# Batch 0's first feed-forward matrix in three token groups inside its own attention, with the weights loaded earlier and the scores ordered anew

## The chip, the cores and the metric

The kernel runs on one core of one Trainium2 chip. The time is that of the device, in microseconds (us), from start to end of one execution. Other numbers come from the profile of one execution of each kernel.

Names of the engines: PE is the tensor engine (matmuls), DVE the vector engine, ACT the scalar engine, POOL the GpSimd engine, SP the engine that issues most DMAs here. A **step** is one pass of the kernel's main loop and handles two score tiles. There are 180 steps, 22.5 for each of 8 batches.

## The reference, cut to what matters

```python
# q, k, v: (8, 12, 448, 64); w_pre, w_post: (12, 12)
scores = q @ k.T / 8                       # per batch and head, 448 x 448
scores = einsum('bhij,hg->bgij', scores, w_pre)     # mix the heads
attn = softmax(scores)
attn = einsum('bhij,hg->bgij', attn, w_post)        # mix the heads again
x = (attn @ v) as (3584, 768)
h = max(x @ w_in, 0)                       # w_in: 768 x 2048
out = (h * h) @ w_out                      # w_out: 2048 x 768
```

For each batch there is attention, which uses all engines, and then a feed-forward part, which is mostly PE work. Its weights are the same for all batches.

## The kernel before

The main loop software-pipelines the attention. Scores of a block of 120 queries are computed (`s_ps`), evicted to an SBUF tile `S` by ACT and DVE, gathered by DMA into tiles `G` that hold 12 heads x 10 queries, mixed (`m_ps`), exponentiated on ACT (`e_sb`), normalised on POOL (`d`), mixed back and transposed (`at_ps`), and multiplied by V (`ot_ps`). The tile `S` has two buffers, so the first evictions of block n+2 wait for the last gathers of block n. Feed-forward work is "filler": it is put between attention instructions of the *next* batch, at an even rate, because PE and POOL run in program order here.

```python
def ffn1_unit(b, ft):
    ps = bank("h_ps")
    for c2 in range(NPAIR):
        nc.tensor.matmul(ps[:, 0:S], lhsT=w1[...], rhs=xts[b][:, c2, :], ...)
    h2 = ffnp.tile([P, S], BF16, name="h2", tag="h2", bufs=FT + 1)
    hr = ffnp.tile([P, S], F32, name="hr", tag="hr", bufs=2)
    nc.scalar.activation(out=hr[:, :], in_=ps[:, 0:S], func=ACT.Relu)
    nc.gpsimd.tensor_tensor(out=h2[:, :], in0=hr[:, :], in1=hr[:, :], op=ALU.mult)
    h2ts[(b, ft)] = h2
# ... cut ...
for x in range(8):                                    # loads, by tile index
    at_load(9 + 5 * x if x else 8, load_w1, x)
    at_load(52 + 2 * x, load_w2, x)
# ... cut ...
for ds in range(nd + LAG):                            # the steps
    # ... loads due, transposes of the next batch due ...
    for s in now2:
        mix(s)
    fill(share)                                       # some filler
    # ... cut: timed units, each charged to the filler's account (owed) ...
    if old2:
        unmix(old2)
        for b1, t1 in old2:
            # ... cut: attention times V when a part of the tiles is done ...
            if t1 == NT - 1:                          # all of batch b1 done
                at_step(ds + 1, (0, lambda b1=b1: filler.extend(ffn_units(b1))))
    for i in (2 * ds + AHEAD, 2 * ds + AHEAD + 1):
        if i < len(steps):
            gather(steps[i])
    scores_up_to(2 * ds + AHEAD + 2)
    fill(share)
```

The softmax here doesn't subtract the row's maximum and nothing guards it: scores larger than these inputs give would overflow.

Of the kernel before, what the change touches and what calls it, by code (L numbers as in the profile page):

```python
# [36 lines left out]
TURN = {0: (6, 8), 1: (7, 8 + LAG), B: (2, 8 + LAG)}  # L37
# [4 lines left out]
def kernel(  # L42
# [24 lines left out]


# [155 lines left out]
    def ffn1_unit(b, ft):  # L224
        ps = bank("h_ps")
        for c2 in range(NPAIR):
            nc.tensor.matmul(ps[:, 0:S], lhsT=w1[ft // 4][:, c2, ft % 4 * 128:ft % 4 * 128 + 128], rhs=xts[b][:, c2, :],  # L227
                             start=(c2 == 0), stop=(c2 == NPAIR - 1))
        h2 = ffnp.tile([P, S], BF16, name="h2", tag="h2", bufs=FT + 1)
        hr = ffnp.tile([P, S], F32, name="hr", tag="hr", bufs=2)  # L230
        nc.scalar.activation(out=hr[:, :], in_=ps[:, 0:S], func=ACT.Relu)  # L231
        nc.gpsimd.tensor_tensor(out=h2[:, :], in0=hr[:, :], in1=hr[:, :], op=ALU.mult)  # L232
        h2ts[(b, ft)] = h2
# [38 lines left out]
    def ffn_units(b):  # L272
        u = [(1140, lambda ft=ft: ffn1_unit(b, ft)) for ft in range(FT)]
        for mt, nt in [(mt, nt) for mt in range(3) for nt in range(2)] + [(3, 0)]:
            for part in range(2):
                u.append((1310, lambda mt=mt, nt=nt, part=part: ffn2_unit(b, mt, nt, part)))
        return u
# [3 lines left out]
    def score_burst(b, blk, pairs):  # L281

        if (b, blk) not in Sb:
            Sb[(b, blk)] = work.tile([P, H, S], BF16, name="S", tag="S", bufs=2)
        sb = Sb[(b, blk)]
        got = []
        for p in pairs:
            for hh in range(2):
                rs = slice(64 * hh, 64 * hh + 64)
                ps = bank("s_ps")  # L290
                nc.tensor.matmul(ps[:, 0:S], lhsT=qTs[b][rs, p, BLK_START[blk]:BLK_START[blk] + P],  # L291
                                 rhs=kTs[b][rs, p, :], start=True, stop=True)
                got.append((2 * p + hh, ps))
        for h, ps in got:
            if h % 2 == 0 or (b == 0 and h in (3, 9)):
                nc.scalar.copy(out=sb[:, h, :], in_=ps[:, 0:S])  # L296
            else:
                nc.vector.tensor_copy(out=sb[:, h, :], in_=ps[:, 0:S])  # L298
# [14 lines left out]
    def mix(s):  # L313
        n = rows_of(s[1])
        ps = bank("m_ps")
        nc.tensor.matmul(ps[:, 0:S], lhsT=pre[0:n, :], rhs=Gs.pop(s)[0:n, :], start=True, stop=True)  # L316
        e = work.tile([P, S], F32, name="e_sb", tag="E", bufs=3)
        sm = work.tile([P, 1], F32, name="sm", tag="sm", bufs=4)
        nc.scalar.activation(out=e[:, :], in_=ps[:, 0:S], func=ACT.Exp, scale=SCALE, accum_out=sm[:, 0:1])  # L319
        rc = work.tile([P, 1], F32, name="rc", tag="rc", bufs=4)  # L320
        nc.vector.reciprocal(out=rc[:, :], in_=sm[:, :])  # L321
        d = dts[(NT * s[0] + s[1]) % ND]
        nc.gpsimd.tensor_scalar(out=d[:, 0:S], in0=e[:, :], scalar1=rc[:, 0:1], scalar2=-1.0 / S,  # L323
                                op0=ALU.mult, op1=ALU.add)
        dsb[s] = d
# [50 lines left out]
    with tc.manual_schedule(engines={PE, POOL}):  # L376
        for x in range(4):
# [3 lines left out]
            if x > 0:  # L381
                score_burst(0, 0, [2 * x - 2, 2 * x - 1])
        for x in range(2):
            score_burst(0, 1, [3 * x, 3 * x + 1, 3 * x + 2])
        for x in range(AHEAD):
            gather(steps[x])
# [5 lines left out]

        for x in range(3):
            load_v(0, x)
            at_load(48 + x, load_v, 1, x)
        for x in range(6):
            at_load(3 * x - 6 if x > 1 else -1, load_qk, 1, x)
            at_load([45, 46, 47, 53, 55, 57][x], load_qk, 2, x)
        for x in range(8):
            at_load(9 + 5 * x if x else 8, load_w1, x)  # L400
            at_load(52 + 2 * x, load_w2, x)
# [9 lines left out]
        issued = [2 * NPAIR]  # L411

        def scores_up_to(tile):
# [3 lines left out]
            size = starts[blk + 1] - starts[blk]  # L417
            want = NPAIR * (blk + 1) + -(-NPAIR * (tile - starts[blk]) // size)
            while issued[0] < want:
                score_burst(*blocks[issued[0] // NPAIR], [issued[0] % NPAIR])  # L420
                issued[0] += 1

        for f in loads.get(-1, []):
            f()
        for ds in range(nd + LAG):
# [12 lines left out]
            rest = ((NT + 1) // 2 + LAG - ds) % (NT / 2) + 1  # L438
            share = sum(w for w, _ in filler) / rest / 2 if now2 else 1e9
            now = timed.pop(ds, [])  # L440
            for s in now2:
                mix(s)
# [4 lines left out]
            if old2:  # L447
                unmix(old2)
                for b1, t1 in old2:
                    ends = PARTS[b1 % 2]  # L450
                    if t1 + 1 in ends:
                        for u in av_units(b1, ends.index(t1 + 1) - 1):
                            at_step(ds + 1, u)
                    if t1 == NT - 1:
                        at_step(ds + 1, (0, lambda b1=b1: filler.extend(ffn_units(b1))))
            for i in (2 * ds + AHEAD, 2 * ds + AHEAD + 1):
                if i < len(steps):
                    gather(steps[i])
            scores_up_to(2 * ds + AHEAD + 2)
# [36 lines left out]
```

## Time and profile before

The first three runs took 638.35, 638.35 and 638.39 us.

The first lines are from the profile page: the busy share of the span in 40 slices (tenths; 9 is 90% or more) for PE, then the granted PE clock in tenths of full speed, then the busy share of the DMA engines.

```profile
PE   4558678699999999999999999999999999999897
...
PEclk9675686799999999999999999999999999999899
DMA  9884869997655785578646885488543655432002
```

There are two regimes. In the first eight slices (to about 128 us) PE is below 90% busy and, but for the first slice, below full clock; from there almost to the end it is busy with hardly a break.

The next view is the table of stretches. Its columns are: stretch, length, busy time of PE, PEld (weight loads), DVE, ACT and POOL, each with a count of instructions, then the granted clock, the DMA share and GB/s. The stretches are cut at the starts of POOL's first `d` pass of steps 0, 12, 30, 60 and 179. POOL makes exactly two such passes in a step.

```profile
22.40:64.20 41.80, 28.44 (x373) 14.37 (x374) 23.16 (x63) 22.97 (x72) 20.32 (x32) 0.61 0.68 127
64.20:119.00 54.80, 36.91 (x505) 17.59 (x504) 35.69 (x96) 33.11 (x104) 35.53 (x54) 0.73 0.94 164
119.00:219.80 100.80, 99.61 (x1260) 53.27 (x1259) 71.86 (x176) 71.04 (x211) 75.92 (x106) 0.98 0.72 130
219.80:581.60 361.80, 355.49 (x4697) 194.43 (x4694) 265.86 (x668) 253.91 (x769) 248.09 (x355) 1.00 0.60 112
581.60:637.80 56.20, 49.23 (x387) 28.37 (x385) 9.74 (x18) 10.78 (x24) 16.15 (x18) 0.95 0.15 43
```

From step 30 on PE is busy 99 and 98% of the time. There, PE work taken away is time saved. In steps 12 to 30 it is busy 67% (36.91 of 54.80) at a clock of 0.73.

The timeline of PE shows its long stops (the first is before step 12, the others are in steps 12 to 30; columns: start, length, engine, line, operation; in brackets PE's idle time before it and what ended it):

```profile
49.40 0.96 PE L162 MATMUL tr_ps<-ident,qst 112*64 112x112 bf16 x16 [6.66 <-ACT S L296]
...
81.12 3.41 PE L181 MATMUL ot_ps<-at,v 112*64 112x160 bf16 x48 [5.89 <-ACT S L296]
...
118.25 0.58 PE L344 MATMUL at_ps<-post,d 60*128 60x60 bf16 x16 [5.22 <-ACT S L296]
...
119.28 2.42 PE L227 MATMUL h_ps<-xt,w 128*128 128x448 bf16 x6
```

PE stands still three times for 5 to 7 us until ACT evicts a score into `S` (L296). The chain of work that ended last has a gather in front of each such eviction (5.11 us before the first, 3.83 and 9.29 us before the others). The last of them (start, length, what):

```profile
108.28 9.29 DMA G<-S
...
117.66 0.54 ACT S L296
```

And the first feed-forward matmul (L227) comes only at 119.28 us: until then none is put between the attention instructions.

### The profile page before, as it was taken

The numbers are of one execution on the slowest core, as the hardware profiler recorded it, in microseconds if no ns is written. First come the engines' busy times: TensorE is split into PE (matmuls) and PEld (weight loads), VectorE is DVE, ScalarE is ACT, GpSimd is POOL, SyncE is SP. The second block draws the span as 40 slices with busy tenths as digits, with TensorE's granted clock in tenths as the row PEclk, the third lists the DMA queues.
The fourth block names the chain that finished last, engine by engine and source line by source line (L and its number), as shares of the span: only waits on it lengthen the run. The fifth ranks groups of instructions, "written<-read, shape, count | busy, mean of one in ns | idle before, by whom it ended". The sixth has DMA issues, their size and how long they took to land.

```text
span 637.8 us, 19148 instructions
## 1 busy us (share of the span) xinstructions
PE 580.7 (91%) x7338; PEld 313.8 (49%) x7338; DVE 414.9 (65%) x1050; ACT 403.5 (63%) x1196; POOL 405.7 (64%) x583
## 2 busy tenths in 40 slices
PE   4558678699999999999999999999999999999897
PEld 3125234345555456455555455545555555555454
DVE  3366666566777767777787677776787677755101
ACT  3656567477467865887578756886587757862330
POOL 6343558699448963888468943897387746873350
PEclk9675686799999999999999999999999999999899
DMA  9884869997655785578646885488543655432002
GB/s 135 141 170 85 153 108 197 197 187 111 139 113 89 127 150 121 92 110 136 140 103 106 135 157 104 87 135 135 126 94 74 110 128 103 81 61 64 25 7 81
DMA packets 90880, 73.61 MB, mean 115 GB/s; under 512 B 6308, under 2 KB 87716, under 8 KB 90788
## 3 DMA queue, kind: packets, MB, share of 16 engines
q1 hardware_dynamic: 51842, 49.57, 34.6%
q0 software_dynamic: 38816, 22.81, 27.8%
q8 instruction: 57, 0.93, 0.6%
q14 instruction: 35, 0.29, 0.1%
q10 hardware_dynamic: 130, 0.01, 0.0%
HBM read 45.63 MB, written 11.01 MB: 89 GB/s over the span
## 4 chain that ended last, share of the span: by engine, by line
PE 67%; POOL 11%; ACT 8%; DMA 5%; DVE 4%; SPq 2%; issue 2%; ACTq 0%; POOLq 0%; DVEq 0%
PE o_ps L254 23%; PE h_ps L227 18%; PE m_ps L316 9%; PE at_ps L344 6%; PE ot_ps L181 5%; POOL d L323 5%; DMA G<-S 4%; POOL h L232 4%; PE s_ps L291 4%; ACT xt L192 3%; ACT e_sb L319 3%; PE tr_ps L162 2%; SPq L310 2%; DVE at L351 2%; ACT S L296 2%
## 5 line engine op out<-in xcount | busy, mean ns | idle before, releaser
L323 POOL TENSOR_SCALAR d<-e_sb,rc 128x448 bf16<-128x448 f32 x360 | 226.7, 641 | 178.0 <-DVE rc L321 175.3
L351 DVE CAST at<-at_ps 112x480 bf16<-112x480 f32 x352 | 221.3, 669 | 41.7 <-PE at_ps L344 41.1
L319 ACT ACTIVATE e_sb<-m_ps 128x448 f32<-128x448 f32 x360 | 195.4, 556 | 59.2 <-PE m_ps L316 51.0
L227 PE MATMUL h_ps<-xt,w 128*128 128x448 bf16 x768 | 167.0, 357 | 0.2 <-ACT e_sb L319 0.2
L254 PE MATMUL o_ps<-w,h 128*128 128x384 bf16 (+1 forms) x1024 | 162.4, 327 | 2.1 <-POOL h L232 2.1
L296 ACT CAST S<-s_ps 128x448 bf16<-128x448 f32 x200 | 105.9, 550 | 55.7 <-PE s_ps L291 27.4
L232 POOL TENSOR_TENSOR h<-hr 128x448 bf16<-128x448 f32 x128 | 118.4, 931 | 26.9 <-ACT hr L231 26.5
L298 DVE CAST S<-s_ps 128x448 bf16<-128x448 f32 x184 | 110.6, 607 | 16.3 <-DMA G<-S 13.7
L316 PE MATMUL m_ps<-G,pre 120*128 120x448 bf16 x360 | 108.0, 374 | 14.4 <-DMA G<-S 6.2
L254 PEld LDWEIGHTS <-h 128*128 128x128 bf16 (+1 forms) x1024 | 85.4, 100 | 71.2 <-issue 16.8
L321 DVE RECIPROCAL rc<-sm 128x1 f32<-128x1 f32 x360 | 55.8, 159 | 99.1 <-ACT e_sb L319 96.2
L227 PEld LDWEIGHTS <-w 128*128 128x128 bf16 x768 | 71.4, 98 | 76.8 <-issue 17.0
L231 ACT ACTIVATE hr<-h_ps 128x448 f32<-128x448 f32 x128 | 70.4, 550 | 44.1 <-PE h_ps L227 33.7
L344 PEld LDWEIGHTS <-d 60*128 60x128 bf16 x2880 | 54.7, 96 | 75.4 <-issue 54.6
L344 PE MATMUL at_ps<-post,d 60*128 60x60 bf16 x2880 | 76.6, 192 | 8.7 <-ACT S L296 6.0
L291 PE MATMUL s_ps<-kT,qT 64*128 64x448 bf16 x384 | 78.2, 370 | 3.1 <-ACT e_sb L319 1.3
L319 ACT ACTIVATION_READ_ACCUMULATOR e_sb<-m_ps 128x1 f32 x360 | 77.9, 216 | 0.0
L192 ACT ACTIVATE xt<-ot_ps,bvec 128x160 bf16<-128x160 f32 (+3 forms) x144 | 42.8, 392 | 43.5 <-PE ot_ps L181 30.8
L316 PEld LDWEIGHTS <-pre 120*128 120x128 bf16 x360 | 29.6, 99 | 54.3 <-issue 25.1
L181 PE MATMUL ot_ps<-at,v 112*64 112x160 bf16 (+4 forms) x1152 | 46.6, 242 | 9.6 <-ACT S L296 5.9
L261 DVE COPY osb<-o_ps 128x384 f32<-128x384 f32 x48 | 26.4, 551 | 39.0 <-PE o_ps L254 37.9
L181 PEld LDWEIGHTS <-v 112*64 112x64 bf16 x1152 | 43.1, 118 | 14.8 <-issue 12.0
(35 smaller groups left out, 189.7 us busy)
## 6 DMA issues: line engine op xcount, KB each, us to landing
G<-S SPq DMA_DIRECT2D x352, 105.0 KB
kst<-in_k_dram POOLq DMA_DIRECT2D x24, 224.0 KB, 5.9
qst<-in_q_dram POOLq DMA_DIRECT2D x24, 224.0 KB, 5.5
v<-in_v_dram POOLq DMA_DIRECT2D x24, 224.0 KB, 6.6
w<-in_moe_w_in_dram POOLq DMA_DIRECT2D x8, 384.0 KB, 6.5
w<-in_moe_w_out_dram POOLq DMA_DIRECT2D x8, 384.0 KB, 9.6
out_dram<-osb SPq DMA_DIRECT2D x8, 336.0 KB
out_dram<-osb SPq DMA_DIRECT2D x8, 288.0 KB
```

What stands on the lines that cost most here:

```text
L181: nc.tensor.matmul(ps[64 * hh:64 * hh + 64, TW * y + c0:TW * y + 2 + n], lhsT=vs[b][0:PR, g, r, :], rhs=at[0:PR, r, g, c0:2 + n], start=(y ...
L227: nc.tensor.matmul(ps[:, 0:S], lhsT=w1[ft // 4][:, c2, ft % 4 * 128:ft % 4 * 128 + 128], rhs=xts[b][:, c2, :], start=(c2 == 0), stop=(c2 = ...
L232: nc.gpsimd.tensor_tensor(out=h2[:, :], in0=hr[:, :], in1=hr[:, :], op=ALU.mult)
L254: nc.tensor.matmul(dst, lhsT=h2ts[(b, ft)][:, mt * 128:mt * 128 + ROWS[mt]], rhs=w2[ft // 4][:, ft % 4, n2 * 384:(n2 + 1) * 384], start=(f ...
L291: nc.tensor.matmul(ps[:, 0:S], lhsT=qTs[b][rs, p, BLK_START[blk]:BLK_START[blk] + P], rhs=kTs[b][rs, p, :], start=True, stop=True)
L296: nc.scalar.copy(out=sb[:, h, :], in_=ps[:, 0:S])
L298: nc.vector.tensor_copy(out=sb[:, h, :], in_=ps[:, 0:S])
L316: nc.tensor.matmul(ps[:, 0:S], lhsT=pre[0:n, :], rhs=Gs.pop(s)[0:n, :], start=True, stop=True)
L319: nc.scalar.activation(out=e[:, :], in_=ps[:, 0:S], func=ACT.Exp, scale=SCALE, accum_out=sm[:, 0:1])
L323: nc.gpsimd.tensor_scalar(out=d[:, 0:S], in0=e[:, :], scalar1=rc[:, 0:1], scalar2=-1.0 / S, op0=ALU.mult, op1=ALU.add)
L344: nc.tensor.matmul(us[y][:, c:c + HR], lhsT=d[rows, PR * r:PR * r + P], rhs=post[rows, :], start=True, stop=True)
L351: nc.vector.tensor_copy(out=dst[:, :, :, y, :], in_=src)
```

## The change

The intent is to give the opening some of batch 0's feed-forward work. Attention times V of batch 0 is finished in three parts of 160, 160 and 128 tokens; after each part the first feed-forward matrix runs for these tokens. For that the weights must come earlier, batch 1's Q and K later. Scores are issued after a small delay and before the gathers of the same step. Both kernels use eight single PSUM banks; only the order in which they are used differs.

```diff
-TURN = {0: (6, 8), 1: (7, 8 + LAG), B: (2, 8 + LAG)}
+FIRST_TURN = (15, 17)
+TURN = {0: FIRST_TURN, 1: (7, 8 + LAG), B: (2, 8 + LAG)}
+EARLY = [10, 18, 25]
 ... cut ...
-    def ffn1_unit(b, ft):
+    def ffn1_unit(b, ft, c0=0, c1=S):
 ... cut: six matmuls over columns c0:c1 ...
-        nc.scalar.activation(out=hr[:, :], in_=ps[:, 0:S], func=ACT.Relu)
-        nc.gpsimd.tensor_tensor(out=h2[:, :], in0=hr[:, :], in1=hr[:, :], op=ALU.mult)
+        if n < S and ft % 2:
+            nc.vector.tensor_scalar_max(out=hr[:, 0:n], in0=ps[:, 0:n], scalar1=0.0)
+        else:
+            nc.scalar.activation(out=hr[:, 0:n], in_=ps[:, 0:n], func=ACT.Relu)
+        nc.gpsimd.tensor_tensor(out=h2ts[(b, ft)][:, c0:c1], in0=hr[:, 0:n], in1=hr[:, 0:n], op=ALU.mult)
 ... cut: scores by pairs (in batch 0 two more of twelve evictions on DVE); both mixing matmuls of a step before its exponentials;
     block 1's scores inside the loop ...
+            at_load(-1 if x < 4 else x - 4, load_w1, x)
+            at_load(20 + 2 * x, load_w2, x)
-            load_v(0, x)
+            at_load(4 + x, load_v, 0, x)
-            at_load(3 * x - 6 if x > 1 else -1, load_qk, 1, x)
+            at_load(8 + 2 * x, load_qk, 1, x)
-            at_load(9 + 5 * x if x else 8, load_w1, x)
-            at_load(52 + 2 * x, load_w2, x)
 ... cut ...
-            size = starts[blk + 1] - starts[blk]
-            want = NPAIR * (blk + 1) + -(-NPAIR * (tile - starts[blk]) // size)
+            if blk == 3:
+                want = NPAIR * 4 + 2 * max(0, ds - FIRST_TURN[1])
+            else:
+                into, size = tile - starts[blk] - 2, starts[blk + 1] - starts[blk] - 2
+                want = NPAIR * (blk + 1) + -(-NPAIR * into // size)
 ... cut ...
+                        if b1 == 0:
+                            c = (IQ * ends[part], min(IQ * ends[part + 1], S))
+                            at_step(ds + 1, (0, lambda c=c: filler.extend(ffn1_units(0, *c))))
 ... cut ...
-            for i in (2 * ds + AHEAD, 2 * ds + AHEAD + 1):
-                if i < len(steps):
-                    gather(steps[i])
-            scores_up_to(2 * ds + AHEAD + 2)
+            scores_for(ds)
+            gathers_for(ds)
```

More of the change, by code (lines that the diff above doesn't have):

```diff
@@ L222, in load_w2 @@
                             in_=moe_w_out[n * x:n * x + n, :].rearrange("(c p) m -> p c m", p=P))
-    def ffn1_unit(b, ft):
+    def ffn1_unit(b, ft, c0=0, c1=S):
         ps = bank("h_ps")
+        n = c1 - c0
         for c2 in range(NPAIR):
-            nc.tensor.matmul(ps[:, 0:S], lhsT=w1[ft // 4][:, c2, ft % 4 * 128:ft % 4 * 128 + 128], rhs=xts[b][:, c2, :],
-                             start=(c2 == 0), stop=(c2 == NPAIR - 1))
-        h2 = ffnp.tile([P, S], BF16, name="h2", tag="h2", bufs=FT + 1)
+            nc.tensor.matmul(ps[:, 0:n], lhsT=w1[ft // 4][:, c2, ft % 4 * 128:ft % 4 * 128 + 128],
+                             rhs=xts[b][:, c2, c0:c1], start=(c2 == 0), stop=(c2 == NPAIR - 1))
+        if (b, ft) not in h2ts:
+            h2ts[(b, ft)] = ffnp.tile([P, S], BF16, name="h2", tag="h2", bufs=FT + 1)
         hr = ffnp.tile([P, S], F32, name="hr", tag="hr", bufs=2)
-        nc.scalar.activation(out=hr[:, :], in_=ps[:, 0:S], func=ACT.Relu)
-        nc.gpsimd.tensor_tensor(out=h2[:, :], in0=hr[:, :], in1=hr[:, :], op=ALU.mult)
-        h2ts[(b, ft)] = h2
+        if n < S and ft % 2:
[3 more added lines that the diff above has]
+        nc.gpsimd.tensor_tensor(out=h2ts[(b, ft)][:, c0:c1], in0=hr[:, 0:n], in1=hr[:, 0:n], op=ALU.mult)
     o_open, osbs = {}, {}
@@ L270, in ffn2_unit, with ffn1_units, ffn2_units @@
                                   in_=osb[64 * n2:64 * n2 + 64, :])
-    def ffn_units(b):
-        u = [(1140, lambda ft=ft: ffn1_unit(b, ft)) for ft in range(FT)]
+    def ffn1_units(b, c0=0, c1=S):
+        return [(int(2.54 * (c1 - c0)), lambda ft=ft: ffn1_unit(b, ft, c0, c1)) for ft in range(FT)]
+    def ffn2_units(b):
+        u = []
         for mt, nt in [(mt, nt) for mt in range(3) for nt in range(2)] + [(3, 0)]:
@@ L279, with score_pair @@
     Sb, Gs, dsb = {}, {}, {}
-    def score_burst(b, blk, pairs):
+    def score_pair(b, blk, p):
         if (b, blk) not in Sb:
             Sb[(b, blk)] = work.tile([P, H, S], BF16, name="S", tag="S", bufs=2)
-        sb = Sb[(b, blk)]
-        got = []
-        for p in pairs:
-            for hh in range(2):
-                rs = slice(64 * hh, 64 * hh + 64)
-                ps = bank("s_ps")
-                nc.tensor.matmul(ps[:, 0:S], lhsT=qTs[b][rs, p, BLK_START[blk]:BLK_START[blk] + P],
-                                 rhs=kTs[b][rs, p, :], start=True, stop=True)
-                got.append((2 * p + hh, ps))
-        for h, ps in got:
-            if h % 2 == 0 or (b == 0 and h in (3, 9)):
-                nc.scalar.copy(out=sb[:, h, :], in_=ps[:, 0:S])
-            else:
-                nc.vector.tensor_copy(out=sb[:, h, :], in_=ps[:, 0:S])
+        pss = [bank("s_ps") for _ in range(2)]
+        for hh in range(2):
+            rs = slice(64 * hh, 64 * hh + 64)
+            nc.tensor.matmul(pss[hh][:, 0:S], lhsT=qTs[b][rs, p, BLK_START[blk]:BLK_START[blk] + P],
+                             rhs=kTs[b][rs, p, :], start=True, stop=True)
+        for hh, copy in enumerate((nc.scalar.copy, nc.vector.tensor_copy)):
+            copy(out=Sb[(b, blk)][:, 2 * p + hh, :], in_=pss[hh][:, 0:S])
     def rows_of(t):
@@ L311, in gather, with mix @@
         Gs[s] = g
-    def mix(s):
-        n = rows_of(s[1])
-        ps = bank("m_ps")
-        nc.tensor.matmul(ps[:, 0:S], lhsT=pre[0:n, :], rhs=Gs.pop(s)[0:n, :], start=True, stop=True)
-        e = work.tile([P, S], F32, name="e_sb", tag="E", bufs=3)
-        sm = work.tile([P, 1], F32, name="sm", tag="sm", bufs=4)
-        nc.scalar.activation(out=e[:, :], in_=ps[:, 0:S], func=ACT.Exp, scale=SCALE, accum_out=sm[:, 0:1])
-        rc = work.tile([P, 1], F32, name="rc", tag="rc", bufs=4)
-        nc.vector.reciprocal(out=rc[:, :], in_=sm[:, :])
-        d = dts[(NT * s[0] + s[1]) % ND]
-        nc.gpsimd.tensor_scalar(out=d[:, 0:S], in0=e[:, :], scalar1=rc[:, 0:1], scalar2=-1.0 / S,
-                                op0=ALU.mult, op1=ALU.add)
-        dsb[s] = d
+    def mix(pair):
+        pss = [bank("m_ps") for _ in pair]
+        for ps, s in zip(pss, pair):
+            n = rows_of(s[1])
+            nc.tensor.matmul(ps[:, 0:S], lhsT=pre[0:n, :], rhs=Gs.pop(s)[0:n, :], start=True, stop=True)
+        for ps, s in zip(pss, pair):
+            e = work.tile([P, S], F32, name="e_sb", tag="E", bufs=3)
+            sm = work.tile([P, 1], F32, name="sm", tag="sm", bufs=4)
+            nc.scalar.activation(out=e[:, :], in_=ps[:, 0:S], func=ACT.Exp, scale=SCALE, accum_out=sm[:, 0:1])
+            rc = work.tile([P, 1], F32, name="rc", tag="rc", bufs=4)
+            nc.vector.reciprocal(out=rc[:, :], in_=sm[:, :])
+            d = dts[(NT * s[0] + s[1]) % ND]
+            nc.gpsimd.tensor_scalar(out=d[:, 0:S], in0=e[:, :], scalar1=rc[:, 0:1], scalar2=-1.0 / S,
+                                    op0=ALU.mult, op1=ALU.add)
+            dsb[s] = d
     def place_of(s):
@@ L381 @@
             if x > 0:
-                score_burst(0, 0, [2 * x - 2, 2 * x - 1])
-        for x in range(2):
-            score_burst(0, 1, [3 * x, 3 * x + 1, 3 * x + 2])
-        for x in range(AHEAD):
-            gather(steps[x])
+                score_pair(0, 0, 2 * x - 2)
+                score_pair(0, 0, 2 * x - 1)
         nc.gpsimd.dma_start(out=wpost_bf[:, :], in_=w_post[0:H, 0:H])
@@ L391, in at_load @@
             loads.setdefault(i, []).append(lambda: f(*args))
+        for x in range(8):
+            at_load(-1 if x < 4 else x - 4, load_w1, x)
+            at_load(20 + 2 * x, load_w2, x)
         for x in range(3):
-            load_v(0, x)
+            at_load(4 + x, load_v, 0, x)
             at_load(48 + x, load_v, 1, x)
         for x in range(6):
-            at_load(3 * x - 6 if x > 1 else -1, load_qk, 1, x)
+            at_load(8 + 2 * x, load_qk, 1, x)
             at_load([45, 46, 47, 53, 55, 57][x], load_qk, 2, x)
-        for x in range(8):
-            at_load(9 + 5 * x if x else 8, load_w1, x)
-            at_load(52 + 2 * x, load_w2, x)
         for b in range(1, B):
@@ L410, with scores_for @@
         starts = [NT * b + TPB * blk for b, blk in blocks] + [len(steps)]
-        issued = [2 * NPAIR]
-        def scores_up_to(tile):
+        issued, gathered = [NPAIR], [0]
+        def scores_for(ds):
+            tile = 2 * ds + AHEAD + 2
             blk = sum(tile >= x for x in starts) - 1
@@ L416, in scores_up_to, with gathers_for @@
                 return
-            size = starts[blk + 1] - starts[blk]
-            want = NPAIR * (blk + 1) + -(-NPAIR * (tile - starts[blk]) // size)
-            while issued[0] < want:
-                score_burst(*blocks[issued[0] // NPAIR], [issued[0] % NPAIR])
-                issued[0] += 1
+            if blk == 3:
[3 more added lines that the diff above has]
+                want = NPAIR * (blk + 1) + -(-NPAIR * into // size)
+            while issued[0] < min(want, NPAIR * (blk + 2)):
+                score_pair(*blocks[issued[0] // NPAIR], issued[0] % NPAIR)
+                issued[0] += 1
+        def gathers_for(ds):
+            while gathered[0] < min(2 * ds + AHEAD + 2, len(steps)):
+                b, t = steps[gathered[0]]
+                if issued[0] < NPAIR * (4 * b + t // TPB + 1):
+                    break
+                gather(steps[gathered[0]])
+                gathered[0] += 1
+        gathers_for(-1)
         for f in loads.get(-1, []):
@@ L438 @@
             rest = ((NT + 1) // 2 + LAG - ds) % (NT / 2) + 1
+            if ds <= EARLY[2]:
+                rest = 1 + min(x for x in EARLY if x >= ds) - ds
             share = sum(w for w, _ in filler) / rest / 2 if now2 else 1e9
             now = timed.pop(ds, [])
-            for s in now2:
-                mix(s)
+            if now2:
+                mix(now2)
             fill(share)
@@ L451 @@
                     if t1 + 1 in ends:
-                        for u in av_units(b1, ends.index(t1 + 1) - 1):
+                        part = ends.index(t1 + 1) - 1
+                        for u in av_units(b1, part):
                             at_step(ds + 1, u)
+                        if b1 == 0:
+                            c = (IQ * ends[part], min(IQ * ends[part + 1], S))
+                            at_step(ds + 1, (0, lambda c=c: filler.extend(ffn1_units(0, *c))))
                     if t1 == NT - 1:
-                        at_step(ds + 1, (0, lambda b1=b1: filler.extend(ffn_units(b1))))
-            for i in (2 * ds + AHEAD, 2 * ds + AHEAD + 1):
-                if i < len(steps):
-                    gather(steps[i])
-            scores_up_to(2 * ds + AHEAD + 2)
+                        if b1 > 0:
+                            at_step(ds + 1, (0, lambda b1=b1: filler.extend(ffn1_units(b1))))
+                        at_step(ds + 1, (0, lambda b1=b1: filler.extend(ffn2_units(b1))))
+            scores_for(ds)
+            gathers_for(ds)
             if ds + 1 < nd + LAG:
```

## The prediction

> **What bounds the kernel now.** Two regimes. From 120 to 582 us the tensor engine (PE) is the limit: the table of stretches shows it 97 to 99% busy at full clock, and the chain of waits is nearly all PE. A step (two score tiles) costs 3.1 us there (149 steps in 463 us). Between 20 and 120 us PE is busy 59 to 74% at a granted clock of 0.57 to 0.76, because batch 0 has attention only; its first feed-forward matmul starts at 119.3 us (timeline of PE), at step 31. There the chain is the gather of scores (22%), its issue (11%), and score evictions waiting for a gather to free their buffer: PE stands still 6.7, 5.9, 3.3 and 5.2 us at block boundaries. DMA is 67 to 76% busy from 20 to 100 us, over 100% until 140 us.
>
> **What the change moves.** No new bank layout (eight single banks are there already). PE's order shows the point: batch 0's first feed-forward matrix, 16 units of six 448-column matmuls (19.4 us for 96 in the tail), becomes 48 units of 160, 160 and 128 columns, started at step 13, half way through the third group by step 31. So about 15 of its 19 us leave the PE-bound part. Tail and steady state keep their work.
>
> **What it adds.** 192 more matmuls. By the Trainium skill ("TensorE: Matmul & The Clock Gate", Back-to-back issue gap) 160 columns need about 70 ns, estimate 0.42 us a unit, the same columns in total; weight loads hide (48 transposes with theirs take 1.30 us here). 32 more squares on POOL (estimate 0.4 us each against 0.93 for 448); half of the small relus go to DVE. Second weights load by tile 34 rather than from tile 52; first weights run ahead of V and batch 1's Q and K, so the first gathers share DMA with 2.3 MB. Score evictions come about one step later, which loosens the wait on their buffer.
>
> **Sum.** Steps 13 to 31 now take 57 us (62 to 119), with 14 us of PE stalls. Per step they will need an estimated 2.4 us of PE, 2.6 of DVE, 2.9 of POOL (two 0.64 us passes, 0.9 of squares, 0.75 of DMA issue): 50 to 55 us, filling what was stall. The start may lose 0 to 4 us to weight traffic; the stall at 112 us should go. Step 31 then falls at 112 to 121 us, I take 117. Total: 638 - 15 - 2 to 4 = 619 us; range 608 to 629. A higher clock in the opening helps a little. Chances: faster by over 2% 0.83, within 2% 0.14, slower 0.03.
>
> **What would show it.** First feed-forward matmul at 60 to 68 us; PE busy over 80% and clock over 0.85 from 65 to 120 us; step 31 within 112 to 121 us; step 33 to the end about 15 us shorter; the last 55 us unchanged; DMA 0.8 to 1.0 until 100 us, lower from 100 to 140 us.
>
> **What would make it wrong.** Gathers delayed by weight traffic (landing over 6 us) so that boundaries stall longer; POOL becoming the limit and holding the small relus; batch 1, lighter on PE, limited by DVE or gathers at over 2.7 us a step, so that saved PE time turns idle; or the other way, the looser score schedule removing nearly all stalls: 605.

## The result, and the profile after

The changed kernel took 629.19 us (median of 4 runs, 628.08 to 629.88), the one before 638.37 us (4 runs, 638.35 to 640.97). The ratio is 0.9845, 95% interval 0.9816 to 0.9873: 1.5% faster, which counts as "the same within 2%". Ratios here are the mean time of one kernel's fast runs over that of the other's of the same rounds, so not quite the ratio of the medians quoted.

The same three views after the change, first the page:

```profile
PE   4467898889999999999999999999999999999897
...
PEclk9666998999999999999999999999999999999899
DMA  9999959679547964587556964587543755322002
```

Then the table of stretches, cut at the same steps:

```profile
24.80:61.80 37.00, 27.41 (x296) 12.21 (x296) 23.85 (x67) 23.97 (x75) 24.99 (x39) 0.62 1.04 190
61.80:118.80 57.00, 50.45 (x838) 34.97 (x837) 43.86 (x121) 37.93 (x124) 48.61 (x90) 0.94 0.87 150
118.80:205.60 86.80, 83.41 (x1210) 46.69 (x1209) 70.54 (x182) 63.07 (x196) 62.62 (x96) 1.00 0.68 123
205.60:570.30 364.70, 357.55 (x4698) 195.26 (x4697) 267.91 (x668) 253.75 (x769) 248.14 (x357) 1.00 0.60 112
570.30:626.30 56.00, 49.03 (x387) 28.88 (x385) 9.74 (x18) 10.75 (x24) 16.14 (x18) 0.97 0.15 43
```

| stretch | before, us | after, us | difference | predicted |
|---|---|---|---|---|
| start to step 0 | 22.4 | 24.8 | +2.4 | 0 to +4 |
| steps 0 to 12 | 41.8 | 37.0 | -4.8 | } |
| steps 12 to 30 | 54.8 | 57.0 | +2.2 | } all three: -2 to -4 |
| steps 30 to 60 | 100.8 | 86.8 | -14.0 | -15 |
| steps 60 to 179 | 361.8 | 364.7 | +2.9 | 0 |
| step 179 to the end | 56.2 | 56.0 | -0.2 | 0 |
| sum | 637.8 | 626.3 | -11.5 | -17 to -19 |

The profiled runs differ by 11.5 us and the medians by 9.2, because the profiled run of before was 1.2 us above its first median and that of after 1.1 us below its own. The stretches tell where the time went: the moved work is saved (14.0 us), the opening as a whole gave nothing (119.0 against 118.8 us at step 30), and the PE-bound stretch lost 2.9 us.

The cut at step 30 matters. There the kernel before has run no feed-forward matmul yet. Its step from 30 to 31 takes 5.0 us, and holds the first two full-size feed-forward units (119.28 to 121.49 us and 122.24 to 124.01 us in the timeline of PE); after the change that step takes 2.2 us. So one step later the changed kernel is 3.1 us ahead (121.0 against 124.1 us). That is part of the moved work, and it is booked here under steps 30 to 60.

The timeline of PE after the change:

```profile
49.51 0.53 PE L295 MATMUL s_ps<-kT,qT 64*128 64x448 bf16 x1 [5.03 <-ACT S L298]
...
60.96 0.57 PE L228 MATMUL h_ps<-xt,w 128*128 128x160 bf16 x6 [0.17 <-ACT e_sb L321]
...
86.54 0.99 PE L228 MATMUL h_ps<-xt,w 128*128 128x160 bf16 x12
87.37 0.54 PE L317 MATMUL m_ps<-G,pre 120*128 120x448 bf16 x2
```

Feed-forward starts at 60.96 us. One long stop before an eviction is left (5.03 us; a shorter one of 2.50 us is at 33.78 us); the ones near 81 and 118 us are gone. Twelve matmuls of 160 columns occupy PE for 0.83 us before the next begins (86.54 to 87.37), 69 ns each. The prediction took about 70 from the Trainium skill ("TensorE: Matmul & The Clock Gate", Back-to-back issue gap). The page gives this as the gap of isolated matmuls and expects more where each has a weight load, about 81 ns for 128 columns; here each has one, and matmuls of 128 columns start 56 ns apart (median of 86 pairs after 80 us), so this trace agrees with the formula and not with the 81 ns. The same page's Part 1 says that the clock is throttled by default and that activity releases it; this trace agrees, the clock of steps 12 to 30 rose from 0.73 to 0.94.

So PE does not stand still as before, and yet steps 12 to 30 take 57.0 us. The waits in that stretch (columns: who waited for whom, us in total, times, longest):

```profile
ACT hr L236 <- POOL h L237: 7.1, 9, 1.3
DVE hr L234 <- POOL h L237: 6.6, 8, 2.0
ACT e_sb L321 <- POOL d L325: 6.1, 7, 1.3
```

The small relus, on ACT and on DVE, wait for POOL to square an earlier one, because the relu output `hr` has two buffers; exponentials wait for POOL's `d` pass for the same kind of reason, with three buffers. The chain that ended last runs on POOL for stretches like this one (start, length, what):

```profile
61.75 1.26 POOL d L325 x2
63.01 0.42 POOL h L237
63.42 0.71 POOL w L221
...
65.41 0.86 POOL h L237 x2
66.27 0.71 POOL w L221
...
67.02 1.25 POOL d L325 x2
```

Two `d` passes, one or two squares and the issue of one weight load, in turn. Over all of steps 12 to 30 POOL has 36% of that chain, PE 23% and the gathers 13%; in a second profile of the same kernel (after_again) POOL has 50%. By the busy groups (count, then busy us and mean ns) a small square is not a third of a large one. Between 60 and 200 us, before and then after:

```profile
L232 POOL TENSOR_TENSOR h<-hr 128x448 bf16<-128x448 f32 x22 | 20.3, 928 | 2.6 <-ACT hr L231 2.6
```

```profile
L237 POOL TENSOR_TENSOR h<-hr 128x160 bf16<-128x160 f32 x32 | 14.0, 448 | 1.0 <-DVE rc L323 0.9
L237 POOL TENSOR_TENSOR h<-hr 128x448 bf16<-128x448 f32 x10 | 9.3, 932 | 0.7 <-ACT hr L236 0.7
L237 POOL TENSOR_TENSOR h<-hr 128x128 bf16<-128x128 f32 x16 | 6.2, 398 | 1.4 <-DVE rc L323 1.3
```

Two squares of 160 columns and one of 128 take 448 + 448 + 398 = 1294 ns where one of 448 took about 930.

### The profile page after: what moved, and what is told of

Read it like the earlier page. It is cut to its first block, busy times and chain, and to the rows that moved or that the text cites. A ratio compares the mean times of both kernels' runs of the same rounds, so it can differ in the third digit from the quotient of the medians.

```text
span 626.3 us, 19617 instructions
## 1 busy us (share of the span) xinstructions
PE 576.3 (92%) x7530; PEld 323.1 (52%) x7530; DVE 423.2 (68%) x1082; ACT 396.7 (63%) x1196; POOL 410.6 (66%) x615
## 4 chain that ended last, share of the span: by engine, by line
PE 61%; POOL 15%; ACT 7%; DVE 6%; DMA 5%; issue 3%; SPq 2%; ACTq 0%; DVEq 0%; POOLq 0%
PE o_ps L258 22%; PE h_ps L228 16%; PE m_ps L317 8%; POOL d L325 6%; PE at_ps L346 5%; POOL h L237 5%; PE ot_ps L181 4%; PE s_ps L295 4%; ACT e_sb L321 3%; ACT xt L192 3%; DMA G<-S 3%; DVE at L353 2%; PE tr_ps L162 2%; DVE S L298 2%; SPq L310 2%
## 5 line engine op out<-in xcount | busy, mean ns | idle before, releaser
L228 PE MATMUL h_ps<-xt,w 128*128 128x448 bf16 (+2 forms) x960 | 168.5, 317 | 2.8 <-ACT e_sb L321 1.6
L237 POOL TENSOR_TENSOR h<-hr 128x448 bf16<-128x448 f32 (+2 forms) x160 | 123.9, 781 | 28.5 <-ACT hr L236 25.8
L228 PEld LDWEIGHTS <-w 128*128 128x128 bf16 x960 | 82.8, 98 | 77.7 <-issue 20.9
L298 ACT CAST S<-s_ps 128x448 bf16<-128x448 f32 x192 | 100.0, 550 | 28.2 <-PE s_ps L295 19.9
L323 DVE RECIPROCAL rc<-sm 128x1 f32<-128x1 f32 x360 | 54.9, 159 | 91.8 <-ACT e_sb L321 89.5
L298 DVE CAST S<-s_ps 128x448 bf16<-128x448 f32 x192 | 112.8, 609 | 5.2 <-PE s_ps L295 2.9
L317 PE MATMUL m_ps<-G,pre 120*128 120x448 bf16 x360 | 104.6, 366 | 12.6 <-DMA G<-S 8.7
L236 ACT ACTIVATE hr<-h_ps 128x448 f32<-128x448 f32 (+2 forms) x136 | 68.5, 504 | 46.8 <-PE h_ps L228 31.0
L295 PE MATMUL s_ps<-kT,qT 64*128 64x448 bf16 x384 | 73.6, 370 | 12.4 <-ACT S L298 7.5
L346 PE MATMUL at_ps<-post,d 60*128 60x60 bf16 x2880 | 75.0, 190 | 4.3 <-ACT xt L192 0.9
```

The lines of the kernel that those rows point to most:

```text
L228: nc.tensor.matmul(ps[:, 0:n], lhsT=w1[ft // 4][:, c2, ft % 4 * 128:ft % 4 * 128 + 128], rhs=xts[b][:, c2, c0:c1], start=(c2 == 0), stop=( ...
L236: nc.scalar.activation(out=hr[:, 0:n], in_=ps[:, 0:n], func=ACT.Relu)
L237: nc.gpsimd.tensor_tensor(out=h2ts[(b, ft)][:, c0:c1], in0=hr[:, 0:n], in1=hr[:, 0:n], op=ALU.mult)
L295: nc.tensor.matmul(pss[hh][:, 0:S], lhsT=qTs[b][rs, p, BLK_START[blk]:BLK_START[blk] + P], rhs=kTs[b][rs, p, :], start=True, stop=True)
L298: copy(out=Sb[(b, blk)][:, 2 * p + hh, :], in_=pss[hh][:, 0:S])
L317: nc.tensor.matmul(ps[:, 0:S], lhsT=pre[0:n, :], rhs=Gs.pop(s)[0:n, :], start=True, stop=True)
```

## The experiments

Twelve kernels ran, with their own runs of before. Steps are compared in the profiled runs. The table has all of them; "12 to 30" and "60 to 179" are the times between those steps in us, from unrounded starts, so they can differ by 0.1 from the stretches shown. How well they repeat: the four kernels with the change's opening (the change, after_again, thin_w2, old_order_late) reach step 30 at 118.8 to 120.4 us, take 57.0 to 57.9 us for steps 12 to 30, and 143.9 to 144.3 us for steps 12 to 60. So a difference of 1 to 2 us in the step 30 column alone says little.

| kernel | median, us | before, us | ratio (95%) | step 30 at | 12 to 30 | 60 to 179 |
|---|---|---|---|---|---|---|
| before | - | - | - | 119.0 | 54.9 | 361.8 |
| the change | 629.19 | 638.37 | 0.9845 (0.9816 to 0.9873) | 118.8 | 57.0 | 364.6 |
| undo_scores | 634.28 | 638.82 | 0.9932 (0.9901 to 0.9963) | 126.2 | 62.4 | 362.3 |
| only_scores | 638.02 | 638.82 | 0.9988 (0.9933 to 1.0042) | 110.5 | 49.4 | 364.1 |
| debt_cleared | 635.61 | 638.82 | 0.9945 (0.992 to 0.997) | 118.0 | 56.3 | 361.4 |
| thin_w2 (wrong result) | 629.44 | 638.82 | 0.9858 (0.9834 to 0.9881) | 120.1 | 57.4 | 364.4 |
| no_groups | 636.58 | 640.85 | 0.992 (0.9871 to 0.9968) | 111.0 | 48.0 | 364.4 |
| hr3 | 626.87 | 640.85 | 0.9773 (0.9758 to 0.9789) | 118.6 | 55.8 | 364.5 |
| squares_dve | 624.8 | 640.85 | 0.9747 (0.9726 to 0.9767) | 114.6 | 53.1 | 364.5 |
| scores_later | 632.19 | 640.85 | 0.9874 (0.9841 to 0.9907) | 116.8 | 55.8 | 368.4 |
| after_again | 629.45 | 639.15 | 0.9838 (0.9812 to 0.9863) | 120.4 | 57.3 | 364.4 |
| old_order_late | 627.85 | 639.15 | 0.9806 (0.9778 to 0.9835) | 120.1 | 57.9 | 362.2 |
| best_dve | 622.12 | 639.15 | 0.9718 (0.9694 to 0.9742) | 115.9 | 53.5 | 362.1 |
| best_act | 621.21 | 639.15 | 0.97 (0.9674 to 0.9726) | 115.7 | 52.8 | 362.1 |

Two theories of the opening stood against each other: **D**, it is bound by DMA traffic (97% busy over the first 118 us after the change), and **E**, it is held by the engines, POOL first. For the PE-bound stretch, theory **S** said that the new order of scores and gathers costs time there; its rival was that something else the change leaves behind does.

### Without the new score order: undo_scores

The score and gather order of before, all else as changed. Batch 1's first block keeps its special place, since its Q and K come late; here that makes seven pairs of scores come at once in step 17, where the change has six.

```diff
-                into, size = tile - starts[blk] - 2, starts[blk + 1] - starts[blk] - 2
-                want = NPAIR * (blk + 1) + -(-NPAIR * into // size)
+                size = starts[blk + 1] - starts[blk]
+                want = NPAIR * (blk + 1) + -(-NPAIR * (tile - starts[blk]) // size)
...
-            scores_for(ds)
-            gathers_for(ds)
+            gathers_for(ds)
+            scores_for(ds)
```
(and block 1's scores before the loop again)

> The change, with only the score and gather order put back to that of before (scores two tiles earlier, spread over the whole block, block 1 before the loop). Theory S: the new order costs 2 to 3 us in the PE-bound part (steps 51 to 179 took 2.9 us longer after the change than before) and gains little in the opening: expect 625 to 627 us, 2 to 3 under the change. Rival: the new order is worth several us in the opening because score evictions no longer wait for gathers, and without it the time is 631 to 635 us.

634.28 us, about 5 us slower than the change: as a total, the rival was right. But both halves can be read off: step 30 comes 7.4 us later (126.2), and steps 60 to 179 take 362.3 us in place of 364.6. The new order is worth a lot in the opening and costs something later. Part of the 7.4 us may be due to the larger bunch in step 17, and against the control (after_again) it is 5.8 us, so the next run is the cleaner one for the opening.

### The score order alone: only_scores

The kernel before with the score functions, the pairing and the loop order of the change; no token groups, loads as before. The edit is the score part of the change's diff, without the special case of block 3.

> The kernel before with only the new score and gather order and the paired mixing matmuls; no token groups, loads as before. Theory S: opening 0 to 3 us shorter, PE-bound part 2 to 3 us longer, so 637 to 640 us, the same as before. Rival: the looser order alone removes most of the PE stalls of the opening (21 us at four block boundaries before): 628 to 633 us.

638.02 us, ratio 0.9988: no gain, as theory S said of the total, but not for its reason. Step 30 comes at 110.5 us, 8.5 us earlier than before. By step 33 all but 0.9 us of it is gone (130.7 us against 131.6). The chain that ended last has one large piece between 108 and 135 us:

```profile
104.83 19.37 DMA qst<-in_q_dram
```

The opening runs ahead, and then the load of a part of batch 2's Q takes 19.37 us, in the time when the second weights are being loaded. The new load order takes the second weights out of that stretch, and in no_groups, which has it too, 4.7 us of gain are left at step 60 (215.1 us against 219.8; 219.9 here). The profiled run here was the slowest of four that spread widely (633.54 to 641.95 us), so how much of the gain the others kept is not shown. Steps 60 to 179 take 364.1 us: the cost of the new order shows again, in a kernel that has neither groups nor new loads.

### Starting the feed-forward earlier without splitting it: debt_cleared

```diff
-                        at_step(ds + 1, (0, lambda b1=b1: filler.extend(ffn_units(b1))))
+                        at_step(ds + 1, (0, lambda b1=b1: arrive(b1)))
...
+    def arrive(b):
+        if b == 0:
+            owed[0] = 0.0
+        filler.extend(ffn_units(b))
```

> The kernel before with one line: the filler's debt (about 7.5 us of transposes and attention-times-V charged while no feed-forward work existed) is set to zero when batch 0's feed-forward arrives, so it starts at step 26 instead of 31, unsplit. If the gain of the change comes from starting batch 0's feed-forward earlier in whatever form, this gets a part of it: 632 to 635 us. If only the split by attention part matters: 637 to 639 us.

635.61 us, ratio 0.9945: a third of the change's gain (0.55 of 1.55%) from one reset in the scheduler's account, as the first theory said in kind (it expected 632 to 635 us). Before, batch 0's filler was available from step 25, but started at the end of step 30 because other work had been charged to it before any filler existed; here it starts in step 26, at 102.3 us.

### Taking away DMA traffic: thin_w2

The second weights are loaded by the same eight instructions, but 16 of 768 columns each. The rest is set to zero once, so the result is wrong.

```diff
-        nc.gpsimd.dma_start(out=w2[x // 2][:, c:c + 2, :],
-                            in_=moe_w_out[n * x:n * x + n, :].rearrange(...))
+        nc.gpsimd.dma_start(out=w2[x // 2][:, c:c + 2, 0:16],
+                            in_=moe_w_out[n * x:n * x + n, 0:16].rearrange(...))
```

> The change, wrong result on purpose: the eight loads of the second weights are issued as before but bring 16 of 768 columns, the rest is set to zero once. Theory D: the opening of the changed kernel is bound by DMA traffic (97% busy over the first 118 us): step 31 comes 6 to 14 us earlier (104 to 112 us) and the total falls by 4 to 10 us, to 619 to 625 us. Rival E: the opening is held by the engines (POOL squares, ring of two relu buffers, DVE): step 31 moves by less than 3 us, total 626 to 630 us.

629.44 us, step 30 at 120.1 us. The table of stretches for steps 12 to 30:

```profile
62.70:120.10 57.40, 50.96 (x839) 35.05 (x837) 44.17 (x121) 38.01 (x124) 48.48 (x89) 0.94 0.66 107
```

The DMA share fell from 0.87 to 0.66 and the stretch took 57.40 us in place of 57.00. Theory D falls for the steps in which these loads run: from 60 to 100 us the share is 0.13 to 0.77 in slices of 5 us, and the steps come no earlier. So the busy share of the DMA engines did not show what held this stretch. That fits the Trainium skill ("Perfetto Trace Analysis", Identifying the Most-Contended Engine), which calls the occupancy of 16 DMA engines misleading. The run does not test the first 60 us, where the first weights load, nor 100 to 115 us, where the share is still 1.0 to 1.1.

### Loads and score order without the groups: no_groups

```diff
-                        if b1 == 0:
-                            c = (IQ * ends[part], min(IQ * ends[part + 1], S))
-                            at_step(ds + 1, (0, lambda c=c: filler.extend(ffn1_units(0, *c))))
...
-                        if b1 > 0:
-                            at_step(ds + 1, (0, lambda b1=b1: filler.extend(ffn1_units(b1))))
+                        at_step(ds + 1, (0, lambda b1=b1: filler.extend(ffn1_units(b1))))
...
-            if ds <= EARLY[2]:
-                rest = 1 + min(x for x in EARLY if x >= ds) - ds
```

> The change without the token groups: new load order and new score order, batch 0's feed-forward unsplit behind the whole attention of batch 0, as before. Theory G (the gain is feed-forward work moved into the opening, the rest only makes room for it): 634 to 640 us; the opening is short (step 30 at 108 to 113 us), but nothing fills it. Rival (the order of the loads and scores is what gains): 626 to 632 us.

636.58 us, with step 30 at 111.0 us: both in the ranges of theory G. But before took 640.85 us on this chip, so the ratio is 0.992 (0.9871 to 0.9968): the loads and the score order alone give 0.8 of the change's 1.55%, about half, and "the rest only makes room for it" is too strong. Without groups, steps 12 to 30 take 48.0 us; with them 57.0. The groups thus cost 9 us of opening and save what the later steps then need not do. The 14 us that leave the PE-bound part are real, but they are not free.

### One more relu buffer: hr3

```diff
-        hr = ffnp.tile([P, S], F32, name="hr", tag="hr", bufs=2)
+        hr = ffnp.tile([P, S], F32, name="hr", tag="hr", bufs=3)
```

> The change with three relu buffers in place of two. Theory E1 (in steps 13 to 30 the small relus on ACT and DVE wait for POOL to square the one before, 14 us of waits between 60 and 120 us, because the ring of two is full): those waits fall by half or more, step 30 comes 2 to 4 us earlier, total 625 to 627 us. Rival E2 (POOL is simply short of time, so a longer ring only queues more): waits move, total 628 to 630 us, unchanged.

626.87 us. The waits in steps 12 to 30:

```profile
ACT e_sb L321 <- POOL d L325: 8.5, 9, 1.7
...
DVE hr L234 <- POOL h L237: 3.4, 3, 2.0
ACT hr L236 <- POOL h L237: 3.0, 7, 0.8
```

The relus' waits fell from 13.7 to 6.4 us, by more than half, as E1 said. But steps 12 to 30 shortened by only 1.2 us (55.8), step 30 did not come 2 to 4 us earlier, and the exponentials now wait longer for POOL (8.5 against 6.1 us), as E2 said. From step 12 to step 60 the gain is clearer: 141.5 us, where the four kernels with the change's opening take 143.9 to 144.3. The ring is a part of the cause. This kernel ran on a chip where before took 640.85 us, so its ratio flatters it; against the two controls (629.19 and 629.45 us on other chips) it is about 2.4 us faster.

### Taking squares off POOL: squares_dve

```diff
         if n < S and ft % 2:
-            nc.vector.tensor_scalar_max(out=hr[:, 0:n], in0=ps[:, 0:n], scalar1=0.0)
+            hs = ffnp.tile([P, 160], BF16, name="hs", tag="hs", bufs=2)
+            nc.vector.tensor_scalar_max(out=hs[:, 0:n], in0=ps[:, 0:n], scalar1=0.0)
+            nc.vector.tensor_tensor(out=h2ts[(b, ft)][:, c0:c1], in0=hs[:, 0:n], in1=hs[:, 0:n], op=ALU.mult)
+            return
```

> The change, with the 24 small relus of DVE also squared on DVE, in bf16 and in buffers of their own: POOL loses 24 of 48 small squares (24 times 0.40 to 0.45 us, some 10 us). Theory E (POOL, 86% busy from 62 to 119 us, holds the opening): step 30 comes 3 to 8 us earlier, total 622 to 627 us. Rival: DVE (77% busy there, plus some 5 us) or PE (88% busy) takes its place at once: 628 to 631 us.

624.8 us, on the same chip as hr3, with step 30 at 114.6 us, 4.2 earlier (5.8 against the control): theory E is borne out, and its rival, that DVE or PE takes POOL's place at once, is not. Steps 12 to 30:

```profile
61.50:114.60 53.10, 48.55 (x840) 33.90 (x838) 47.94 (x141) 37.47 (x124) 41.26 (x71) 0.97 0.89 158
```

POOL's busy time fell by 7.4 us (48.61 to 41.26), DVE's rose by 4.1, and the stretch lost 3.9 us. The DMA share went *up*. Removing bytes had moved nothing and removing POOL work moved the stretch by about half of the work removed. This edit also takes the odd relus out of the ring of two, so it removes both the work and a part of the coupling; hr3, which loosens the coupling alone, gives 1.2 of the 3.9 us in steps 12 to 30, and 2.4 of 3.7 us in steps 12 to 60 (141.5 and 140.2 us against 143.9). The two shares are not separated further.

### Scores later still: scores_later

```diff
-                into, size = tile - starts[blk] - 2, starts[blk + 1] - starts[blk] - 2
+                into, size = tile - starts[blk] - 4, starts[blk + 1] - starts[blk] - 4
```

> The change with the scores one more step later (four tiles into the block in place of two, spread over the rest). If the wait of the first score evictions of a block for the last gathers of the block before the last is what the new order loosens (undoing it cost 5 us), a further step loosens it more in the opening: step 30 comes 1 to 4 us earlier, total 625 to 628 us. Rival: the wait is gone already, and the scores bunched into four steps delay the gathers: 629 to 634 us.

632.19 us, about 3 us more than the change took on other chips (the intervals of the two ratios overlap): the rival's range. The opening did gain 2 us (step 30 at 116.8), as the first theory said, though that is little more than the profiles spread; steps 60 to 179 took 368.4 us, far outside their spread. With the delay of before, of the change, and of this kernel, that stretch takes 361.4 to 362.3, 364.1 to 364.6 and 368.4 us: the later the scores, the slower the PE-bound part. This edit changes the delay alone; what the swap of scores and gathers within a step adds was not tested apart.

### The control, and the old order late: after_again and old_order_late

after_again is the changed kernel, unedited, for comparison on the same chip with the three kernels that follow.

> The changed kernel once more, unedited, as the control for the three others on the same chip (its partner ran at 638.4 us in the first comparison, 638.8 and 640.9 us in the next two). Expect a ratio of 0.982 to 0.987; if it is near 0.975 the gains read for the relu ring and for the squares on DVE were mostly the chip's.

629.45 us and 0.9838, as expected: the first comparison repeats. old_order_late keeps the new order up to step 22 and has the old one from step 23.

```diff
+OLD_FROM = 23
...
-                into, size = tile - starts[blk] - 2, starts[blk + 1] - starts[blk] - 2
+                late = 0 if ds >= OLD_FROM else 2
+                into, size = tile - starts[blk] - late, starts[blk + 1] - starts[blk] - late
...
-            scores_for(ds)
-            gathers_for(ds)
+            for f in ((gathers_for, scores_for) if ds >= OLD_FROM else (scores_for, gathers_for)):
+                f(ds)
```

> The change with the new score and gather order kept up to step 22 and that of before from step 23 on. Theory S: steps 60 to 179 take 361 to 362.5 us as in the three kernels with the old order, not the 364 to 365 us of those with the new one, and the total falls by 2 to 3 us against the control. Rival (the extra time there comes from something else that the groups or loads leave behind): 364 us and no change of the total.

627.85 us. Steps 60 to 179 in the table of stretches:

```profile
206.40:568.60 362.20, 356.18 (x4697) 194.74 (x4696) 265.98 (x667) 253.47 (x769) 247.41 (x356) 1.00 0.60 112
```

362.20 us against 364.70 for the change, with the opening, groups and loads left as they were. Theory S is confirmed for the stretch, which is what it was about. The totals' medians differ by 1.6 us, less than the 2 to 3 expected, and the intervals of the two ratios overlap, so by totals alone it would not be settled. What exactly costs the time under the new order stays open: PE's busy time is 1.4 us shorter here than after the change and its idle time (length less busy time) 1.1 us shorter. One wait goes with the order. In this stretch, after the change and then here, ACT waits for the mixed scores:

```profile
ACT e_sb L321 <- PE m_ps L317: 45.6, 35, 2.3
```

```profile
ACT e_sb L322 <- PE m_ps L318: 37.3, 34, 2.3
```

It is 45 to 47 us in the kernels with the change's order, 36 to 39 us in those with the old one, and 49.9 us in scores_later. Whether it is a cause or a consequence is not shown.

### Everything together: best_dve and best_act

best_dve joins three edits: the old order from step 23, the odd small squares on DVE, three relu buffers. best_act is the same with the square on ACT:

```diff
-            nc.vector.tensor_tensor(out=h2ts[(b, ft)][:, c0:c1], in0=hs[:, 0:n], in1=hs[:, 0:n], op=ALU.mult)
+            nc.scalar.activation(out=h2ts[(b, ft)][:, c0:c1], in_=hs[:, 0:n], func=ACT.Square)
```

> The change with three edits together: old order from step 23, the odd small squares on DVE, three relu buffers. If the two causes are independent: about 4 us from the opening and 2.5 us from the PE-bound part, so 5 to 8 us under the control, ratio to before 0.970 to 0.977, a verdict of faster. If they share a cause: 3 to 4 us under the control.

> As best_dve, but the odd small squares on ACT, which is 71% busy from 60 to 120 us where DVE would be 91% busy. If DVE is what holds the opening next, step 30 comes 1 to 3 us earlier than in best_dve. If PE (92% busy there) holds it, or if the hop from DVE to ACT costs as much as it frees, the same within 1 us or later.

best_dve took 622.12 us, ratio 0.9718, and best_act 621.21 us, ratio 0.97. Both are correct, both are faster than before by over 2%, and best_dve is 7.3 us under the control. Its two rows, steps 12 to 30 and 60 to 179:

```profile
62.50:115.90 53.40, 47.85 (x840) 33.27 (x839) 48.66 (x142) 37.92 (x125) 40.87 (x70) 0.97 0.90 160
202.40:564.50 362.10, 355.64 (x4697) 194.55 (x4696) 265.75 (x667) 253.90 (x769) 247.30 (x355) 1.00 0.60 112
```

The opening's gain (57.3 to 53.5 us) and that of the late stretch (364.4 to 362.1) are both there in full, so the two causes are independent. Within the opening they are not: three relu buffers on top of the squares on DVE add nothing that shows (53.5 us here, 53.1 in squares_dve; steps 12 to 60 take 140.0 and 140.2 us), so hr3 and squares_dve loosen the same hold. best_act reaches step 30 within 0.2 us of best_dve (115.7 against 115.9). So either DVE, 91% busy (48.66 of 53.40) in best_dve, was not what held the opening next, or the hop from DVE to ACT cost as much as it freed; the run cannot tell. What holds it next is open. In the chain that ended last, the gathers of scores are the largest piece of that stretch in both kernels, 35% against 13% after the change; no run tests this.

## Why the prediction was right or wrong

Predicted: 619.0 us, range 608 to 629, with 0.83 for "faster by over 2%". Measured: 629.19 us, 1.5% faster. The median lies 0.2 us above the upper end of the range, and the class that got most of the chance did not come. The moved work came as forecast; two other terms of the sum, the opening and the steady state, missed in the same direction, and the gain was half of that forecast.

- **The moved work: right.** "About 15 of its 19 us leave the PE-bound part": steps 30 to 60 became 14.0 us shorter. The first feed-forward matmul came at 60.96 us (predicted 60 to 68). In steps 12 to 30 PE was 89% busy at a clock of 0.94 (predicted over 80% and over 0.85).
- **The opening: the step that failed.** The prediction put steps 13 to 31 at "50 to 55 us, filling what was stall". They took 57.0 (12 to 30), more than the 54.8 of before, so that the whole opening gave 0.2 us in place of 2 to 4. It took the length of a step as the sum of work on its busiest engine, POOL at 2.9 us a step. POOL was in fact busy 2.7 us a step (48.61 over 18 steps) and PE 2.8 (50.45 over 18, predicted 2.4), but a step took 3.2: ACT and DVE waited 13.7 us for squares and ACT 6.1 us for `d` passes, through rings of two and three buffers. The prediction named this as a risk ("POOL becoming the limit and holding the small relus") and did not charge for it. hr3 and squares_dve show this hold, through the rings and POOL's own work together, to be the cause of about 4 us.
- **"Tail and steady state keep their work": right for the work, wrong for the time.** The tail is unchanged (56.2 and 56.0 us). The steady state lost 2.9 us in the profiled runs, of which old_order_late gives back 2.5. The prediction counted the new score order only as a gain for the opening.
- **The score order's gain: right in sign.** It "loosens the wait on their buffer": only_scores reaches step 30 8.5 us earlier. But that gain was spent on running the groups (no_groups: 48.0 us without, 57.0 with them).
- **Its own marks: one at the edge, one missed.** Step 31 was to fall at 112 to 121 us (117 taken) and came at 121.0. (Its 119 us for step 31 of the kernel before is the start of the first feed-forward matmul, which is step 30 in the tables here; by POOL's marker that kernel's step 31 is at 124.1.) "Step 33 to the end about 15 us shorter" became 8.9 us shorter (506.2 to 497.3): at step 33 the change is 2.6 us ahead, and the steady state gives 2.9 us back later.
- **"The stall at 112 us should go": right.** PE's longest stop after 100 us in the opening is under 1 us after the change. "DMA 0.8 to 1.0 until 100 us" was half right: it was over 1.0 from 20 to 80 us and 0.62 from 80 to 100.
- **"The start may lose 0 to 4 us to weight traffic": right.** Step 0 comes 2.4 us later, and in only_scores, with the loads of before, at 21.4 us.

The sum of the profiled runs is then -0.2 (to step 30) - 14.0 + 2.9 - 0.2 = -11.5 us, against the -17 to -19 predicted: some 3 us of the miss lie in the opening, 3 in the steady state and 1 in the moved work. Another 2.3 us, between the profiled difference and that of the medians, are spread of the runs and are not explained here.

## What to carry to other kernels

Moving work from a bound stretch into an idle one pays only what the idle stretch can take: add up not just each engine's busy time there, but the rings of few buffers through which the slowest engine holds the others, and split small passes with their fixed cost in mind. A gain in one stretch can be thrown away at the next queue (the profiled run of only_scores won 8.5 us and had lost all but 0.9 three steps later), so compare kernels by markers at the same step and not by totals alone. A rule that helps while an engine waits (later scores in the opening) may hurt where another engine is the limit, and can be switched over in between.

The Trainium skill ("Perfetto Trace Analysis", Optimization Strategy) describes the change's idea, interleaving regimes whose most-contended engines differ, and says that consistent bubbles can mean too few buffers. This case agrees with the first (14.0 us saved in steps 30 to 60). On the second, the page speaks of the engine that should be saturated; here the waits were on ACT and DVE (13.7 us on a ring of two), and a third buffer cut them to 6.4 us and saved 2.4 us by step 60.

## What the Trainium skill lacked or had wrong

- "GPSIMD Engine Reference", 3.1 Elementwise: the page gives about 2.6 cycles per element for a two-input pass and no figure for the whole fixed part of an instruction on this engine. Here squares of 128, 160 and 448 columns took 398, 448 and 932 ns. The two larger ones give an estimate of 1.68 ns a column ((932 - 448) / 288), which is 2.0 cycles at the page's 1.2 GHz and so below its 2.6 (these squares read one fp32 tile twice and write bf16), and a fixed part of some 180 ns, which is why three short passes cost 1294 ns and one long one 932. Spans on POOL are rough; by the spacing of starts back to back (362, 416 and 897 ns) the fixed part is some 150 ns.
- "Perfetto Trace Analysis", Optimization Strategy: it advises interleaving regimes and does not say that the work put in has a price in the idle stretch. Here steps 12 to 30 took 48.0 us without the groups and 57.0 with them, for 14.0 us saved later.
